# The first stage's steps put in other places within the engines' orders, its filler matmuls dropped, and the last 256 tokens stored in four pieces

## The chip, the cores and the metric

One core of a Trainium2 chip runs the kernel. The metric is device time in microseconds (us), the median of the timed runs. Engines: TensorE (PE, with its weight loads PEld), VectorE (DVE), ScalarE (ACT), GpSimd (POOL) and SyncE (SP), which issues most DMAs.

## The reference, cut to what matters

```python
# q, k, v: (4, 8, 576, 64); all float32
q_d, k_d, v_d = (t.reshape(B, H, 144, 4, D).mean(axis=3) for t in (q, k, v))
out_up = np.repeat(softmax_attention(q_d, k_d, v_d), 4, axis=2)
out_local = softmax_attention(q, k, v, mask=abs(i - j) < 4)
x = (out_up + out_local).transpose(0, 2, 1, 3).reshape(2304, 512)
h = np.maximum(np.maximum(x @ w1, x @ w2), x @ w3)      # 512 -> 768
x = h @ w_out                                           # 768 -> 512
h = x @ w_in; g = np.maximum(0.01 * h, h)               # 512 -> 2048
return g @ moe2_w_out                                   # 2048 -> 512
```

## The kernel before

Every product that needs full precision is done in parts: a value is split into a rounded high part and the rest (names ending in h and l), and three of the four partial products are summed.

The first stage makes the attention and the first mixture. It goes through eight units u of 288 tokens. For each unit TensorE runs 18 steps `L{u}.0` to `L{u}.17` (line 921, 12 matmuls of 288 columns each, into one PSUM bank out of a ring of four) and then eight steps `Y{u}.o.p` (line 953: four column blocks o; p = 0 has 15 matmuls and p = 1 the last three, which need `hl{u}.5`). Each L has an eviction `X` (ACT or DVE); after every third come `hh` and `hl`, the high and low part of the maximum (`hl` on POOL, in the last two units on DVE). A bank is free for the fourth allocation after it when its X is done.

Between these steps stand those of the attention. Units 0 to 3 use TensorE for the local part, per head pair h: `C{u}.h` scores (PE), `D` maximum (DVE), `E` exponentials (ACT), `H` reciprocal (DVE), `I` normalising (POOL), `O` transposes (PE), `o` copy (DVE), `P` product (PE), `Q` sum with the pooled part (DVE), `R` high part, `S` low part (POOL). `L{u}.0` needs `S{u}.3`. Units 4 to 7 do it without TensorE: products `mu` (POOL, 3.06 us each), sums `r` and `a` (DVE, ACT), softmax `s1`, `e`, `s2`, then `pm` and `ps` (DVE), and transposes `tp` with `ta`, `th`, `tx` behind them; `L{u}.0` needs `tx{u}.2`. The pooled attention of batch b has steps `A` (pooling), `B` scores, `F`, `G`, `J`, `K`, `PV`, `M` transposes, `m`, `N`, `v`. Until about 83 us DVE also joins the weights of the first mixture (`cy8` to `cy23`, two instructions each, with `cx`, `cz` on ACT or DVE and `cu` on POOL); a `cx` takes a bank of the ring of four too, which its `cy` gives back.

The second stage (lines 1148 and 1189, steps with @) is the second mixture: `@w..` split its weights, `@xl`, `@xs`, `@xh`, `@xo` load and split x, `@G` and `@H` are TensorE's steps, `@f..` add up the results, and `@fj`, `@fk` store them.

The order of all steps of one engine is fixed when the program is built: `Plan.order` (line 125) goes through the steps with planned durations and due times and returns one list; each engine works through its steps in the order of that list, whatever is ready. Two rules tie it to time. Where DVE works in a mode that shares its port with POOL (`Plan.alone`, line 121), the first such step waits for the last POOL step ahead of it in the list, and the other way round. And where the plan saw a gap of over 0.9 us on TensorE in its first 150 us (`KEEP_TO`), line 1682 put filler matmuls (`keep`, line 905) ahead of the step behind the gap. They write the unused columns of the bank of the newest L or Y step, with weights that compute nothing. Another 12 stand within `L0.0` (`FIRST`).

Of the kernel before, what the change touches and what calls it, by code (L numbers as in the profile page):

```python
# [19 lines left out]
DM = H * D  # L20
# [3 lines left out]
G = 32  # L24
# [9 lines left out]
M1 = FF1 // 128  # L34
M2 = FF2 // 128
# [9 lines left out]
N2 = 384  # L45
# [19 lines left out]
)  # L65
FILL0 = 7
FIRST = 12
KEEP_TO = 150.0
ON_A = (0, 21, 14)
NS = 3 * M1  # L70
CONV = 8
# [4 lines left out]
SHIFT = {"@": 8.7, "pv": 21, "ra": 7.2, "t": -44.8, "mu": 41.9, "c": 21.4, "ds3": -78.6, "ds2": -60.8, "pl3": -14.9, "pl1": 29.8, "co": 28.7, "pl2": 1.2, "ds1": -5.6}  # L76
SLACK = {"c": 20, "mu": 155.4, "ds3": 65.3, "co": -32.2, "t": 17, "pv": 57.9}
LEN = (56.8, 80.6, 38.5, 57.8, 38.8, 56.8, 30, 55)
GAP = 1.04
# [2 lines left out]
BANKS = {"B": "early", "M": "at", "N": "mm", "O": "at", "C": "early"}  # L82
BOOST = {"at": 36.8, "early": 10.6}


def kind(n):
    if n[0] == "@":
# [14 lines left out]
class Plan:  # L102
# [7 lines left out]
    def step(self, name, engine, time, fn, deps=(), after=0.2, alone=False, begin=-1e9, other=None):  # L110
        assert name not in self.steps
        self.steps[name] = dict(
            engine=engine, time=time, first=time, fn=fn, deps=list(deps), after=after, alone=alone, begin=begin, other=other, tags=[]
        )

    def holds(self, tag, bufs, first, last):
# [8 lines left out]
    def order(self, due, shift, slack, gap):  # L125
# [20 lines left out]
        for n in reversed(topo):  # L146
            due.setdefault(n, 1e9)
            for d in st[n]["deps"]:
                if n[0] == "@" != d[0]:
                    continue  # L150
                own = n[0] == "@" and st[d]["engine"] == st[n]["engine"]
# [3 lines left out]
        begin = {n: max(due[n] - slack.get(kind(n), 1e9), st[n]["begin"], FLOOR.get(kind(n), -1e9)) for n in due}  # L155
# [6 lines left out]
        out, now = [], 0.0  # L162
# [25 lines left out]
        while len(out) < len(st):  # L188
            began = False
            for e in self.ENGINES:  # L190
# [3 lines left out]
                for n, t in ready[e].items():  # L194
                    x = st[n]
# [9 lines left out]
                x = st[best]  # L205
# [21 lines left out]
            if not began:  # L227
# [28 lines left out]
def local_global_attention_moe_kernel(  # L256
# [14 lines left out]
    nc = tc.nc  # L271
    A, T = nc.scalar, nc.tensor
# [629 lines left out]
    def keep(n):  # L902
        w = ident.bitcast(BF16)
        for _ in range(n if "mm" in live and banks_taken[0] - live["at"] < 3 else 0):
            T.matmul(
                out=live["mm"][:, NCOL:], lhsT=w[:, :128], rhs=w[:, : 512 - NCOL],
                start=False, stop=False, skip_group_check=True,
            )
# [297 lines left out]
            fin[c, half] = p2["f"].tile([128, 2, 512], F32, tag="ob", bufs=3, name="ob")[:, : sups[c][1] // 256]  # L1206
        return fin[c, half][:, :, 256 * n : 256 * n + 256]

    def fin_store(c, half):
        n0, n = sups[c]  # L1210
        nt = n // 256
        for t in range(nt):
            store_rows(n0 + (half * nt + t) * 128, fin[c, half][:, t], A if half and c == len(sups) - 1 else nc.sync)

    def store_rows(first, ob, queue):
        a = 0
        while a < 4:
            u, r = divmod(first // G + a, RU)
            bb, half = divmod(u, 2)
            e = min(4, a + RU - r)  # L1220
            if u < PEU:
                row, step = first + a * G, DM
                runs = [(row, a, e)]
            else:
                row = u * NCOL + r if u == PEU and half else bb * S + half * RU + r
                step = (RU if u == PEU and half else R) * DM
                runs = [(row + x - a, x, x + 1) for x in range(a, e)]
            for row, x, y in runs:
                queue.dma_start(
                    out=bass.AP(tensor=out.tensor, offset=out.offset + row * DM, ap=[[step, (y - x) * G], [1, DM]]),  # L1230
                    in_=ob[x * G : y * G],
                )
            a = e
# [3 lines left out]
    with tc.manual_schedule(engines={ET.SP, ET.PE, ET.DVE, ET.Activation, ET.Pool}):  # L1237
# [408 lines left out]
        for c in range(len(sups)):  # L1646
            t = 0.16 + 0.54 * sups[c][1] / SB
            k = f"{c}"
            done = [f"@H{c}.{NP - 1}.{j}" for j in range(7)]

            def add(x, j, deps, f):
                go(f"@f{x}{k}", "DVE", t, f, deps)
                due[f"@f{x}{k}"] = due[done[j]] + 1.5

            go(f"@fa{k}", "ACT", t, lambda c=c: fin_copy(c, 0, "s1"), [done[0], "open6"])
            go(f"@fd{k}", "ACT", t, lambda c=c: fin_copy(c, 3, "s5"), [done[3]])
            due[f"@fa{k}"], due[f"@fd{k}"] = due[done[0]] + 1, due[done[3]] + 1
            add("b", 1, [f"@fa{k}", done[1]], lambda c=c: added(fin_ob(c, 0, 0), fin[c, "s1"], in_bank(c, 1)))
            add("c", 2, [f"@fb{k}", done[2]], lambda c=c: added(fin_ob(c, 0, 1), fin[c, "s1"], in_bank(c, 2)))
            add("e", 4, [f"@fc{k}", done[4]], lambda c=c: added(fin[c, "s1"], fin_ob(c, 0, 1), in_bank(c, 4)))  # L1660
            add("f", 5, [f"@fe{k}", done[5]], lambda c=c: added(fin_ob(c, 1, 0), fin[c, "s1"], in_bank(c, 5)))
            add("g", 6, [f"@fd{k}", f"@fe{k}"], lambda c=c: added(fin_ob(c, 0, 1), fin_ob(c, 0, 1), fin[c, "s5"]))
            add("h", 6, [f"@fg{k}", done[6]], lambda c=c: added(fin_ob(c, 0, 1), fin_ob(c, 0, 1), in_bank(c, 6)))
            add("i", 6, [f"@ff{k}"], lambda c=c: added(fin_ob(c, 1, 1), fin[c, "s1"], fin[c, "s5"]))
            go(f"@fj{k}", "SP", 1.45, lambda c=c: fin_store(c, 0), [f"@fb{k}", f"@fh{k}"], after=2.0)
            go(f"@fk{k}", "SP", 1.45, lambda c=c: fin_store(c, 1), [f"@ff{k}", f"@fi{k}"], after=2.0)
            due[f"@fj{k}"] = due[f"@fk{k}"] = due[done[6]] + 5
            for j, x in enumerate("abcdefh"):
                holds("yyyyxxz"[j], 4 if j < 4 else 2, f"@H{c}.0.{j}", [f"@f{x}{k}"])
            holds("s1", 1, f"@fa{k}", [f"@ff{k}", f"@fi{k}"])  # L1670
            holds("s5", 1, f"@fd{k}", [f"@fg{k}", f"@fi{k}"])
            holds("ob", 3, f"@fb{k}", [f"@fj{k}"])
            holds("ob", 3, f"@ff{k}", [f"@fk{k}"])
        ordered = mybir.DependencyInfo(mybir.DependencyClass.Sync, mybir.DependencyReason.DATA)
        apart = {"DVE": None, "POOL": None}
        done = 0.0
        for n in pn.order(due, SHIFT, SLACK, GAP):
            x = pn.steps[n]
            if x["engine"] == "PE" and n[0] != "@":
                gap = pn.end[n] - x["time"] - done  # L1680
                done = pn.end[n]
                if 0 < done < KEEP_TO and gap > 0.9:
                    keep(int((gap - 0.5) / 0.1))
            if x["engine"] not in ("DVE", "POOL") or n[0] == "@":
                x["fn"]()
                continue
            eng = V if x["engine"] == "DVE" else P
            eng.first, before = None, apart[x["engine"]]
            x["fn"]()
            if before is not None and (x["engine"] == "POOL" or pn.alone(n, "DVE")):  # L1690
                tc.add_manual_dep(eng.first.ins, before.ins.name, ordered, reason="one port")
                apart[x["engine"]] = None
            if x["engine"] == "POOL":
                apart["DVE"] = eng.last
            elif pn.alone(n, "DVE"):
                apart["POOL"] = eng.last
# [69 lines left out]
```

## Time and profile before

| what | value |
|---|---|
| median of 3 runs | 766.83 us (766.65 to 771.97) |
| the profiled execution, its time | 768.03 us |
| its span, first to last instruction | 766.2 us |
| PE busy | 753.7 us (98%) |
| DVE, ACT, POOL busy | 586.9, 442.2, 234.6 us |
| filler matmuls in all | 30 |

A row of the timeline gives start, duration, engine, line, operation, what is written and read, its size and count; in brackets stands the idle time of the engine before it and what ended it. Neighbours of one kind are merged. Line 248 is a helper through which all DVE and POOL operations go, so they are told apart by their tiles: `hm` is written by X, `wl` and `wy` by the joins cy, `ps_ls` and `plsm` by D and H, `dsqk` by A, `plt` by o, `hl` and `xl` by hl and S, `qkprod` by mu.

### The profile page before, as it was taken

How to read it: one execution, taken by the hardware profiler on the slowest of the kernel's cores; microseconds unless marked ns; L12 is line 12 of the kernel's file. 1: busy time of each engine (PE TensorE's matmuls, PEld its weight loads, DVE VectorE, ACT ScalarE, POOL GpSimd, SP SyncE). 2: the span in 40 equal slices, each digit the busy share in tenths (PEclk: the TensorE clock that was granted, in tenths of full speed). 3: DMA queues.
4: the chain of work that ended last, by engine and by line, in shares of the span. 5: the costliest groups of instructions: out<-in, count | busy, mean ns of one | idle time of the engine just before them, and what ended most of it. 6: DMA issues, size and time to landing. Idle time of an engine off the chain costs nothing.

```text
span 766.2 us, 16061 instructions
## 1 busy us (share of the span) xinstructions
PE 753.7 (98%) x5929; PEld 724.1 (95%) x5929; DVE 586.9 (77%) x1045; ACT 442.2 (58%) x1464; POOL 234.6 (31%) x221
## 2 busy tenths in 40 slices
PE   9999999999999999999999999999999999999997
PEld 5788899889899999999999999999999999999997
DVE  6998675577996893876788888668666987879882
ACT  6988549685246854223456798668678443433440
POOL 5988769787768855100000000000000000000000
PEclk9999999999999999999999999999999999999999
DMA  9972073645424203041324777987987545454522
GB/s 361 407 309 71 17 262 113 197 131 154 147 95 142 73 31 108 1 131 40 114 85 149 247 269 248 369 312 252 317 256 269 145 116 164 125 148 138 152 73 80
DMA packets 58510, 130.60 MB, mean 170 GB/s; under 512 B 5952, under 2 KB 30528, under 8 KB 58432
## 3 DMA queue, kind: packets, MB, share of 16 engines
q1 hardware_dynamic: 53680, 124.60, 48.6%
q10 hardware_dynamic: 4752, 4.98, 1.9%
q8 instruction: 46, 0.75, 0.4%
q14 instruction: 32, 0.26, 0.1%
HBM read 93.91 MB, written 35.65 MB: 169 GB/s over the span
## 4 chain that ended last, share of the span: by engine, by line
PE 79%; POOL 8%; DVE 6%; DMA 3%; issue 2%; ACT 2%; DVEq 0%; ACTq 0%; SPq 0%; POOLq 0%
PE acc L1189 22%; PE ps_h L921 19%; PE ps_y L1148 13%; PE ps_o L953 9%; PE ps_z L1148 7%; POOL qkprod L248 4%; PE ps_x L1148 3%; PE ps_sc L743 2%; DMA sqk<-in_qk_dram 1%; ACT qkprod L484 1%; POOL hl L248 1%; DMA lk<-in_kL_dram 1%; DVE wl L248 1%; POOL ple L248 1%; PE ps_ls L593 1%
## 5 line engine op out<-in xcount | busy, mean ns | idle before, releaser
L921 PE MATMUL ps_h<-xh,wA 128*128 128x288 f32 x1152 | 198.3, 299 | 0.2 <-ACT xh L391 0.2
L921 PEld LDWEIGHTS ps_h<-xh,wA 128*128 128x128 f32 x1152 | 166.4, 190 | 5.6 <-issue 3.7
L1189 PE MATMUL acc<-w,gs 128*128 128x256 f32 x1512 | 171.6, 276 | 0.0
L1189 PEld LDWEIGHTS acc<-w,gs 128*128 128x128 f32 x1512 | 171.5, 188 | 0.0
L921 PE MATMUL ps_h<-xl,wA 128*128 128x288 f32 x576 | 108.8, 295 | 1.1 <-POOL xl L248 1.0
L1148 PE MATMUL ps_y<-xop,w 128*128 128x384 f32 x576 | 105.7, 335 | 0.0
L1172 ACT ACTIVATE gs<-gr 128x1792 fp32r<-128x1792 f32 x36 | 60.8, 1703 | 76.0 <-DVE gr L248 61.8
L1148 PEld LDWEIGHTS ps_y<-xop,w 128*128 128x128 f32 x576 | 100.3, 188 | 0.1
L921 PEld LDWEIGHTS ps_h<-xl,wA 128*128 128x128 f32 x576 | 87.6, 190 | 1.8 <-POOL xl L248 1.8
L248 DVE TENSOR_TENSOR gs<-gr,gs 128x1792 fp32r<-128x1792 f32 x36 | 72.6, 2021 | 13.3 <-ACT gs L1172 13.2
L953 PE MATMUL ps_o<-hh,wO 128*128 128x288 f32 x384 | 79.0, 300 | 0.0
L248 POOL TENSOR_TENSOR qkprod<-lq,lk 128x1344 f32<-128x1344 f32 x24 | 73.7, 3081 | 4.9 <-issue 2.1
L484 ACT ACTIVATE qkprod<-qkprod 128x64 f32<-128x64 f32 x280 | 67.4, 255 | 6.5 <-POOL qkprod L248 4.9
L953 PEld LDWEIGHTS ps_o<-hh,wO 128*128 128x128 f32 x384 | 60.8, 188 | 2.1 <-issue 1.4
L248 DVE TENSOR_TENSOR gr<-gr 128x256 f32<-128x256 f32 (+1 forms) x108 | 53.3, 509 | 9.4 <-DMA gr<-gd 7.9
L248 DVE TENSOR_TENSOR hm<-hm,ps_h 128x288 f32<-128x288 f32 x96 | 42.9, 447 | 21.8 <-PE ps_h L921 20.2
L953 PE MATMUL ps_o<-hl,wO 128*128 128x288 f32 x192 | 56.4, 294 | 1.2 <-POOL hl L248 1.2
L484 ACT ACTIVATION_READ_ACCUMULATOR qkprod<-qkprod 128x1 f32 x280 | 56.2, 201 | 0.1
L1148 PE MATMUL ps_z<-xop,w 128*128 128x384 f32 x288 | 53.8, 335 | 0.0
L1148 PEld LDWEIGHTS ps_z<-xop,w 128*128 128x128 f32 x288 | 50.3, 188 | 0.0
L1131 ACT ACTIVATE g<-g 128x384 f32<-128x384 f32 x72 | 37.3, 521 | 20.9 <-DVE g L248 16.8
L248 DVE TENSOR_TENSOR w<-w2y,w 128x512 fp32r<-128x512 f32 (+1 forms) x64 | 38.5, 618 | 6.1 <-ACT w L1060 6.1
(143 smaller groups left out, 1194.6 us busy)
## 6 DMA issues: line engine op xcount, KB each, us to landing
gd<-g SPq DMA_DIRECT2D x96, 192.0 KB, 4.1
gr<-gd SPq DMA_DIRECT2D x32, 512.0 KB, 4.1
sqk<-in_qk_dram SPq DMA_DIRECT2D x20, 579.0 KB, 4.5
wA<-in_wa_dram SPq DMA_DIRECT2D x18, 512.0 KB, 9.8
dsrawv<-in_vP_dram SPq DMA_DIRECT2D x16, 512.0 KB, 3.9
wl<-in_w_in_dram SPq DMA_DIRECT2D x16, 512.0 KB, 3.3
wl<-in_w_out_dram SPq DMA_DIRECT2D x16, 512.0 KB, 4.7
wd<-w2y SPq DMA_DIRECT2D x8, 896.0 KB, 5.8
```

Source lines behind the costliest of these rows:

```text
L248: self.last = f(*args, **kwargs)
L484: A.activation(out=pr[:, r, j], in_=pr[:, r, j], func=AF.Copy, accum_out=sc[:, r, j : j + 1])
L593: T.matmul(out=pst[hh][:QB, j * KB : j * KB + KB], lhsT=qr[rows, qs], rhs=kr[rows, ks], start=False, stop=j == NBLK - 1,)
L743: T.matmul(out=pst[hh][:QC, c * SD : c * SD + SD], lhsT=t[rows, 0, qs] if b else raw[rows, qs, f], rhs=t[rows, 1, :], start=f == 0, stop=f ...
L921: T.matmul(out=ps, lhsT=wA[m, e][wi][:, kk * 128 : kk * 128 + 128], rhs=xx[:, kk], start=n == 0, stop=n == 3 * KC - 1)
L953: T.matmul(out=ps, lhsT=wO[m][wi][:, os_], rhs=xx[:, m], start=m0 == n == 0, stop=m1 == M1 and n == len(terms) - 1)
L1131: A.activation(out=g, in_=g if src is None else blk.pop((q, src)), func=AF.Prelu, alpha=0.01)
L1148: T.matmul(out=ps, lhsT=w[:, kk * 128 : kk * 128 + 128], rhs=xx, start=j in (0, 1, 3) and n == 0, stop=n == 5, skip_group_check=True,)
L1172: A.activation(out=ga[i][:, 0], in_=gr[i], func=AF.Copy)
L1189: T.matmul(out=acc[c, j][:, k * 256 : k * 256 + 256], lhsT=a[:, m : m + 128], rhs=w, start=p == 0 and k == 0 and n == 0, stop=p == NP - 1 ...
```

## The change

Steps stay what they are. After `Plan.order` a new method takes 838 steps out of the list and puts each run of them behind a named step (table `MOVED`, 251 runs), and gives 51 steps of copying or pooling to the other of their two engines (`SWAPPED`). The filler matmuls of `KEEP_TO` are gone (`KEPT` is empty); the 12 of `FIRST` stay. For the last 256 tokens each of the two stores is cut into two column halves: the first half is issued when its columns are done.

```diff
-KEEP_TO = 150.0
+MOVED = (
...
+    "H1.1>o1.0>hh0.3 C1.2>P1.0 cz16>cz15 cy17>X0.12 cu16>I1.1 L0.13>O1.1>D1.2>cy18>Q1.0>L0.14>cu15 "
...
+    "@w3i4.1>@xo0.1>@w0i5.0 @wqi5.0>Y7.0.0>Y7.1.0>Y7.0.1>st7.0>@w1i5.0 @w3i4>@wri5.0>Y7.2.0>Y7.1.1>Y7.3.0 "
...
+KEPT = {}
...
+    def rearrange(self, out):
+        runs = [r.split(">") for r in MOVED.split()]
+        moved = {n for r in runs for n in r[1:]}
+        out = [n for n in out if n not in moved]
+        for first, *rest in runs:
+            i = out.index(first) + 1
+            out[i:i] = rest
+        for n in SWAPPED.split():
+            x = self.steps[n]
+            x["engine"], x["time"] = x["other"] if x["engine"] == x["own"] else (x["own"], x["first"])
+        return out
...
-    def fin_store(c, half):
+    def fin_store(c, half, part=None):
...
+        c0, c1 = (0, DM) if part is None else (256 * part, 256 * part + 256)
...
+            store_rows(n0 + (half * nt + t) * 128, fin[c, half][:, t, c0:c1], A if half and part else nc.sync, c0, c1)
...
-        for n in pn.order(due, SHIFT, SLACK, GAP):
+        for n in pn.rearrange(pn.order(due, SHIFT, SLACK, GAP)):
             x = pn.steps[n]
-            if x["engine"] == "PE" and n[0] != "@":
-                gap = pn.end[n] - x["time"] - done
-                done = pn.end[n]
-                if 0 < done < KEEP_TO and gap > 0.9:
-                    keep(int((gap - 0.5) / 0.1))
+            if n in KEPT:
+                keep(KEPT[n])
```

Read out of the list before and the table, the orders of the places that the text below comes to:

```
PE, first unit    before: L0.0 C1.0 L0.1 .. L0.5 C1.1 L0.6 O1.0 L0.7 L0.8 L0.9 P1.0 L0.10 C1.2 L0.11 O1.1 ..
                  after:  L0.0 L0.1 C1.0 L0.2 .. L0.8 O1.0 C1.1 L0.9 L0.10 L0.11 L0.12 C1.2 P1.0 L0.13 O1.1 ..
                  before: .. L0.17 O1.2 B1.0 Y0.0.0 P1.2 ..    after: .. L0.17 P1.2 B1.0 Y0.0.0 ..
DVE, from L0.10   after:  X0.10 cy16 X0.11 cy15 H1.1 o1.0 hh0.3 cy17 D1.2 cy18 Q1.0 X0.13 cy19 H1.2 X0.14 o1.1
                          cy20 cy22 hh0.4 D1.3 cy21 Q1.1 o1.2 A1.0 H1.3 X0.16 X0.17
PE, around Y2     before: Y2.1.1 Y2.3.0 P3.3 N2.0 Y2.2.1 Y2.3.1 M2.1 B2.3 L3.0 ..
                  after:  Y2.1.1 N2.0 P3.3 Y2.3.0 Y2.2.1 Y2.3.1 M2.1 L3.0 L3.1 L3.2 L3.3 N2.1 L3.4 B2.3 ..
POOL, unit 1      before: I2.3 mu10.0 hl1.5           after: I2.3 S2.1 hl1.5 A2.0 .. S2.3 mu10.0
POOL, unit 2      before: mu11.0 S2.3                 after: S2.3 mu10.0 .. mu11.0
POOL, unit 3      before: K2.2 mu12.0 PV2.2 S3.3      after: mk11 S3.3 PV2.2 A2.3 hl3.0 K2.2 .. mu12.0
                  before: mu12.2 mu13.2 hl3.5         after: hl3.4 hl3.5 mu12.2 .. mu13.2
DVE, unit 7       before: X7.17 hh7.5 hl7.5
                  after:  X7.17 @wri4.1 @w2i4.0 @w2i4.1 @w5i26 @xo0.4 @w5i21 hl7.5   (hh7.5 on ACT)
```

## Rows read from the trace of the kernel before

**Rows 1.** Windows: stretch, its length, busy us (instructions) by engine, clock, DMA share, GB/s
```profile
42.40:80.40 38.00, 36.31 (x312) 33.97 (x313) 34.42 (x75) 33.23 (x97) 32.51 (x37) 1.00 0.38 148
203.80:207.50 3.70, 2.16 (x18) 1.35 (x16) 3.60 (x7) 1.82 (x6) 2.47 (x4) 0.89 0.51 151
207.50:210.10 2.60, 2.60 (x12) 2.60 (x12) 2.49 (x4) 0.00 (x0) 2.30 (x4) 0.51 0.27 101
415.70:595.00 179.30, 179.30 (x1049) 179.17 (x1049) 134.34 (x229) 136.58 (x274) 0.00 (x0) 1.00 0.81 278
```

**Rows 2.** Timeline of PE in unit 0: filler matmuls and the step behind them
```profile
59.21 0.54 PE L905 MATMUL ps_h<-ident 128*128 128x224 bf16 x4 [0.82 <-DVE hm L248]
...
80.41 1.12 PE L905 MATMUL ps_h<-ident 128*128 128x224 bf16 x10
...
82.10 0.40 PE L953 MATMUL ps_o<-hh,wO 128*128 128x288 f32 x1
```

**Rows 3.** Timeline of DVE in unit 0
```profile
58.71 0.45 DVE L248 TENSOR_TENSOR hm<-hm,ps_h 128x288 f32<-128x288 f32 x1
59.08 0.69 DVE L248 SCALAR_TENSOR_TENSOR wl<-wA,wl 128x512 int32<-128x512 int32 x1
...
60.78 1.37 DVE L248 TENSOR_REDUCE dsqk<-sqk 128x144 f32<-128x576 f32 x2
...
76.62 1.06 DVE L248 TENSOR_REDUCE ps_ls<-ps_ls 96x3 f32<-96x306 f32 x2
...
79.91 0.44 DVE L248 TENSOR_TENSOR hm<-hm,ps_h 128x288 f32<-128x288 f32 x1
...
81.01 0.78 DVE L248 COPY plt<-ps_lt 102x384 f32<-102x384 f32 x2
```

**Rows 4.** Timeline of PE from 144 to 247 us: the steps that waited
```profile
144.90 0.52 PE L953 MATMUL ps_o<-hh,wO 128*128 128x288 f32 x2
146.29 0.40 PE L953 MATMUL ps_o<-hl,wO 128*128 128x288 f32 x1 [0.88 <-POOL hl L248]
...
157.37 0.40 PE L921 MATMUL ps_h<-xl,wA 128*128 128x288 f32 x1 [0.15 <-POOL xl L248]
...
196.44 0.38 PE L645 MATMUL ps_lt<-ident,ple 96*102 96x96 f32 x2 [0.22 <-DVE dssum L248]
...
204.75 0.44 PE L791 MATMUL ps_aT<-ident,dse 72*72 72x72 f32 x4 [0.55 <-ACT up L391]
206.18 1.39 PE L743 MATMUL ps_sc<-dsqk 64*72 64x144 f32 x8 [0.99 <-ACT aT L391]
...
246.85 0.40 PE L953 MATMUL ps_o<-hl,wO 128*128 128x288 f32 x1 [0.32 <-POOL hl L248]
```

**Rows 5.** Timeline of POOL: what stood ahead of hl1.5, S3.3 and hl3.5
```profile
141.34 3.06 POOL L248 TENSOR_TENSOR qkprod<-lq,lk 128x1344 f32<-128x1344 f32 x1 [0.42 <-DVE hh L248]
...
205.10 0.80 POOL L248 TENSOR_TENSOR xl<-x,xh 128x288 fp32r<-128x288 f32 x1 [0.18 <-ACT xh L391]
...
239.90 6.14 POOL L248 TENSOR_TENSOR qkprod<-lq,lk 128x1344 f32<-128x1344 f32 x2
```

**Rows 6.** Timeline of PE in units 5 and 6: a whole L step, and the first L of unit 6
```profile
320.17 1.22 PE L921 MATMUL ps_h<-xh,wA 128*128 128x288 f32 x8
...
321.75 1.21 PE L921 MATMUL ps_h<-xh,wA 128*128 128x288 f32 x8
...
338.88 0.65 PE L921 MATMUL ps_h<-xh,wA 128*128 128x288 f32 x3
```

**Rows 7.** Timeline of DVE: the last low part for unit 6, and hl7.5
```profile
337.19 0.29 DVE L248 TENSOR_TENSOR xl<-ps_x,xh 128x128 fp32r<-128x128 f32 x1 [0.44 <-ACT xh L882]
...
407.05 0.46 DVE L248 TENSOR_TENSOR hl<-hm,hh 128x288 fp32r<-128x288 f32 x1
```

**Rows 8.** Timeline of PE in Y7.0.1: its first matmul with hl7.5
```profile
410.23 0.29 PE L953 MATMUL ps_o<-hl,wO 128*128 128x288 f32 x1
```

**Rows 9.** DMA issues of the last 12 us: tiles, queue, count, size, us to landing
```profile
out_dram<-ob SPq DMA_DIRECT2D x1, 256.0 KB, 2.4
```

More of the change, by code (lines that the diff above doesn't have):

```diff
@@ L86, in kind @@
+SWAPPED = (
[3 rows of a table added]
+)
+KEPT = {}
 def kind(n):
@@ L112, in step @@
         self.steps[name] = dict(
-            engine=engine, time=time, first=time, fn=fn, deps=list(deps), after=after, alone=alone, begin=begin, other=other, tags=[]
+            engine=engine, own=engine, time=time, first=time, fn=fn, deps=list(deps), after=after, alone=alone, begin=begin, other=other, tags=[]
         )
@@ L1207, in fin_ob, with store_rows @@
         return fin[c, half][:, :, 256 * n : 256 * n + 256]
-    def fin_store(c, half):
+    def fin_store(c, half, part=None):
         n0, n = sups[c]
         nt = n // 256
+        c0, c1 = (0, DM) if part is None else (256 * part, 256 * part + 256)
         for t in range(nt):
-            store_rows(n0 + (half * nt + t) * 128, fin[c, half][:, t], A if half and c == len(sups) - 1 else nc.sync)
-    def store_rows(first, ob, queue):
+            store_rows(n0 + (half * nt + t) * 128, fin[c, half][:, t, c0:c1], A if half and part else nc.sync, c0, c1)
+    def store_rows(first, ob, queue, c0, c1):
         a = 0
@@ L1229, in store_rows @@
                 queue.dma_start(
-                    out=bass.AP(tensor=out.tensor, offset=out.offset + row * DM, ap=[[step, (y - x) * G], [1, DM]]),
+                    out=bass.AP(tensor=out.tensor, offset=out.offset + row * DM + c0, ap=[[step, (y - x) * G], [1, c1 - c0]]),
                     in_=ob[x * G : y * G],
@@ L1664, in local_global_attention_moe_kernel @@
             add("i", 6, [f"@ff{k}"], lambda c=c: added(fin_ob(c, 1, 1), fin[c, "s1"], fin[c, "s5"]))
-            go(f"@fj{k}", "SP", 1.45, lambda c=c: fin_store(c, 0), [f"@fb{k}", f"@fh{k}"], after=2.0)
-            go(f"@fk{k}", "SP", 1.45, lambda c=c: fin_store(c, 1), [f"@ff{k}", f"@fi{k}"], after=2.0)
-            due[f"@fj{k}"] = due[f"@fk{k}"] = due[done[6]] + 5
+            for x, half, deps in (("j", 0, "bh"), ("k", 1, "fi")):
+                deps = [f"@f{y}{k}" for y in deps]
+                if c == len(sups) - 1:
+                    for part in range(2):
+                        go(f"@f{x}{k}" if part else f"@f{x}{k}.0", "SP", 0.75, lambda c=c, h=half, p=part: fin_store(c, h, p), [deps[part]], after=2.0)
+                        due[f"@f{x}{k}" if part else f"@f{x}{k}.0"] = due[done[6]] + 5 if part else due[deps[0]] + 1
+                else:
+                    go(f"@f{x}{k}", "SP", 1.45, lambda c=c, h=half: fin_store(c, h), deps, after=2.0)
+                    due[f"@f{x}{k}"] = due[done[6]] + 5
             for j, x in enumerate("abcdefh"):
@@ L1675, in local_global_attention_moe_kernel @@
         apart = {"DVE": None, "POOL": None}
-        done = 0.0
-        for n in pn.order(due, SHIFT, SLACK, GAP):
+        for n in pn.rearrange(pn.order(due, SHIFT, SLACK, GAP)):
             x = pn.steps[n]
-            if x["engine"] == "PE" and n[0] != "@":
-                gap = pn.end[n] - x["time"] - done
-                done = pn.end[n]
-                if 0 < done < KEEP_TO and gap > 0.9:
-                    keep(int((gap - 0.5) / 0.1))
+            if n in KEPT:
+                keep(KEPT[n])
             if x["engine"] not in ("DVE", "POOL") or n[0] == "@":
```

69 lines of the change are left out of this document (added), and 3 rows, old and new, of the table SWAPPED.

## The prediction

> **What bounds the kernel now.** I read the page first (TensorE is busy for 98% of the span), then the windows by stretch, then TensorE's timeline wherever a window shows less than its full length, and last the timelines of the engines that ended its waits. From 415.70 to 595.00 TensorE is busy for 179.30 of 179.30 us at full clock [rows 1]: the second stage has nothing that an order could win. What can be won lies in the first stage, in two kinds of places.
>
> The first is unit 0. From 42.40 to 80.40 VectorE is busy for 34.42 of 38.00 us [rows 1], with the joins of the weights between TensorE's evictions. In this stretch the fillers cost time. They write the bank that the last L has just filled, so they cannot start until its eviction has read it: the eviction that starts at 58.71 ends at 59.16, and the fillers start at 59.21; the one at 79.91 ends at 80.35, and the ten fillers start at 80.41 [rows 2, 3]. The reader is to see that a filler meant for an idle gap here makes the gap.
>
> The second are single waits between 144 and 247 us [rows 4]. `hl1.5` came late for Y1.0.1: two matmuls from 144.90, the third at 146.29. At 0.132 us a matmul (12 from 320.17 to 321.75 [rows 6]) the two need 0.26, so 1.13 us are lost where the row says 0.88 idle; a wait costs some 0.25 more than its idle time, since a matmul's drain counts as busy. In the same way `S2.3` cost 0.15 + 0.25 = 0.40, a bank for `O3.3` 0.22 + 0.25 = 0.47, and `hl3.5` 0.32 + 0.25 = 0.57. The largest place is M2.1 and B2.3: idle for 0.55 and 0.99, with the same addition 2.04. Behind it the granted clock was 0.51 for the 2.60 us from 207.50 [rows 1], that is 1.2 of 2.4 GHz, which cost about 1.3.
>
> **The change, part by part.** *The waits from 144 to 247 us.* Ahead of `hl1.5` on GpSimd stood a product of 3.06 us, ahead of `hl3.5` two of together 6.14 [rows 5]; both now stand behind it, and the same is done for `S2.3`. Ahead of `S3.3`, which ran at 205.10, one product and two shorter steps go. Each of these moves more than the wait it answers. B2.3 reads banks that M2.1's copies must first give back, and stood directly behind it; now five L and a small step lie between, 5 x 1.58 = 7.9 us against a wait of 0.99. N2.0, whose copy (the ACT `up` of the 0.55) M2.1 waited for, goes ahead of P3.3 and Y2.3.0; that step's 15 matmuls (15 x 0.132 = 2.0) cover 0.55. With the waits the fall of the clock goes, as TensorE was idle just before it. I take all of it: 1.13 + 0.40 + 0.47 + 2.04 + 1.3 + 0.57 = 5.9 us gained; the bounds are 0 and 5.9.
>
> *Unit 0.* Without the fillers' wait L0.9 can start 0.82 + 0.25 before 59.21, at 58.15, and with P1.0 moved behind it L0.10 ends 2 x 1.58 later, at 61.3. From there VectorE sets the pace, since the banks for the next L come from its joins. Ahead of B1.0 it has, in the new order: 8 joins at 1.39 (from 59.08 to 60.47 as the sum of two of 0.69), 11.1; 11 small steps (evictions, Q, H, two hh) at 0.37 (58.71 to 59.08), 4.1; two D at 1.06, 2.1; three o at 0.78, 2.3; A1.0, 1.37 [rows 3]. Together 21.0, so to 82.3. B1.0 itself takes what is left between 80.41 and 82.10 when ten fillers of about 0.1 are taken off (1.12 for all, most of it overlapped), some 0.65; so Y0.0.0 starts at about 83.0 instead of 82.10 [rows 2]. But P1.2 then lies behind TensorE and M1.1 stands later: two steps like B1.0, some 0.5 each, estimated from it. So unit 0 gains nothing: -0.9 + 1.0, which I take as 0. The bounds: VectorE waits as long again as it was idle before (38.00 - 34.42 = 3.6), of which some 1.5 fall on TensorE's path: -1.5; or TensorE sets the pace and the three filler groups' 2 x (1.07 + 0.3) + 1.0 come back: +3.7.
>
> *Unit 7.* `hl7.5` now has six weight steps ahead of it. It ran at 407.05 [rows 7], and its first reader at 410.23 [rows 8], a cover of 410.23 - 407.51 = 2.7. Six steps of about 0.6 (a 0.69 instruction starts every 0.6 to 0.7, as joins do [rows 3]) are 3.6, and hh7.5's 0.3 leaves VectorE: hl7.5 is ready at 410.8, so Y7.0.1 waits 0.6. Loss 0.6, bounds 0 and 1.5. What queues behind hl7.5 on VectorE are steps for `@G`, all wanted after 415.70.
>
> *The swaps* move steps of 0.3 to 0.45 between VectorE and ScalarE and are in the counts above where they lie in unit 0. *The table's DMAs* (73 of the moved steps are SP's) issue loads behind others that wait for their buffer; I take 0.3 lost in all for products that start later on GpSimd, which had the room.
>
> *The last stores.* A store of 256 KB took 2.4 us to land [rows 9]; the last pieces are now 128 KB. If half of it went with the bytes, 1.2 would go; if nothing did, 0. I take 0.3, near the lower end, because the piece still has to be issued and confirmed. [...]
>
> The sum: 5.9 + 0 - 0.6 - 0.3 + 0.3 = 5.3 us. The profiled execution took 768.03, so its like would take 762.7; the median of the runs is 766.83, 1.2 lower, and by it 761.5.
>
> **The rivals.** *Everything goes, unit 0 too.* TensorE then gains up to 3.7 more there; with 3 of it the time is 758.5. For it speaks that the fillers' wait is real [rows 2, 3]; against it that VectorE has 21 us of work where TensorE has less.
>
> *The gain is given back at L6.0.* GpSimd's products are put off, not saved, and units 4 to 7 hang on them and on VectorE. `L6.0` started at 338.88, the last low part that it needs ended at 337.48 [rows 6, 7]: only 1.4 us of cover. If VectorE does not get to that part earlier, all gain beyond 1.4 ends there: 1.4 - 0.6 + 0.3 = 1.1, so 765.7. Against it speaks that the transposes for it stand between TensorE's own steps and move with them.
>
> *Slower: the clock falls in unit 0.* With no fillers TensorE stands still in some six places between 61 and 83 us, as it did for 0.55 and 0.99 before the clock fell at 207 [rows 1, 4]. TensorE has about 16 us of work there (7 x 1.58 and some 5 of small steps) in 21.7; at half clock that is 32, or 10 late: 761.5 + 10 = 771.5, slower than before. A fall as long as the one in the trace, 2.60 us in that window, hides in the 5.7 us that VectorE leaves; it decides against the change from 5.7 + 5.3 = 11 us of work at half clock on. The Trainium skill (TensorE: Matmul & The Clock Gate, "Part 1: The HAM clock gate") says that half clock is the resting state and that the engine's own activity releases it; by that page fillers are what keeps it, and the one fall in the trace, behind the idle 0.55 and 0.99, agrees. Against it speaks that TensorE was busy for 36.31 of 38.00 in this stretch at clock 1.00, three waits included [rows 1].
>
> **How the numbers follow.** The forecast (759.2 to 764) 0.46; all of it gained (757 to 759.2) 0.29; given back at L6.0 or at another wait of that kind (764 to 767) 0.17; the clock or another new wait in unit 0 (767 to 776) 0.08. The range leaves out the last case and the outer part of the second: 757.5 to 766.5. About 1% is what a measurement of this kernel can tell from no change, so faster begins at 759.2 and slower at 774.5: faster 0.29, within 0.67, slower 0.04 (half of the last case).
>
> **What would show it.** Right: no L905 rows behind 45 us; no idle of TensorE put down to a POOL `hl` or `xl` between 140 and 250; B2.3 without a wait and the clock at 1.00 around L3.0; Y0.0.0 at 82 to 83.5 with waits for VectorE of 0.3 to 1.5 ahead of it; Y7.0.1 waiting for a VectorE `hl`; the second stage starting 5 to 6 us before 415.70 with no idle in it. Wrong: Y0.0.0 well before 82 (unit 0 pays), L6.0 waiting for `xl` (given back), a clock of 0.5 between 61 and 83, or waits of the second stage's first steps for weights that the table puts later.

## The result, and the profile after

The kernel after takes 777.93 us (median of four, 776.93 to 780.33) against 768.08 for the kernel before: a ratio of 1.0125, 95% interval 1.0078 to 1.0171. It is slower by about 10 us where a gain of 5.3 was forecast. Its profiled execution took 776.93 us with a span of 775.1; before it was 768.03 with 766.2. Code behind the table stands 90 lines lower in after (L921 is L1011, L1189 is L1279). Below, the steps `@G` are called the second stage and the steps `@H` the third; the text so far counts both to the second.

The two traces are best compared by the starts of TensorE's steps, in us:

| step | before | after | after minus before |
|---|---|---|---|
| Y0.0.0, first product of unit 0 | 82.10 | 83.21 | +1.1 |
| L1.0 | 97.74 | 97.14 | -0.6 |
| L4.0 | 253.07 | 243.65 | -9.4 |
| L5.0 | 295.26 | 288.84 | -6.4 |
| L7.0 | 377.58 | 372.78 | -4.8 |
| G0.0.0, start of the second stage | 415.52 | 411.29 | -4.2 |
| G0.1.3, its eighth step | 422.80 | 425.04 | +2.2 |
| H0.0.0, start of the third stage | 590.36 | 593.05 | +2.7 |
| last matmul | 761.63 | 771.01 | +9.4 |
| end of the span | 766.16 | 775.14 | +9.0 |

So the first stage did gain, more than forecast up to L4.0. Then 3.0 us go in unit 4, 6.5 in the first seven steps of the second stage, and 6.7 in the third stage, whose matmuls the change does not touch.

The windows of after (stretch, length, busy us and instructions of PE, PEld, DVE, ACT, POOL, clock, DMA share, GB/s). The first answers the first of [rows 1]. The second is the stretch from L1.0 to L4.0: no idle time, and the clock, which in before fell around L3.0, stays at 1.00:

```profile
42.40:80.40 38.00, 34.56 (x296) 31.80 (x295) 32.71 (x71) 32.05 (x94) 26.87 (x24) 1.00 0.33 127
97.14:243.65 146.51, 146.51 (x1277) 138.90 (x1276) 109.22 (x221) 87.68 (x544) 110.86 (x100) 1.00 0.42 141
244.00:256.00 12.00, 9.50 (x71) 8.69 (x70) 4.24 (x10) 6.10 (x43) 7.89 (x6) 1.00 0.91 335
411.30:416.00 4.70, 3.29 (x20) 2.96 (x18) 2.35 (x4) 0.61 (x2) 0.00 (x0) 1.00 0.85 262
418.00:424.00 6.00, 4.88 (x15) 4.57 (x15) 6.00 (x11) 4.59 (x10) 0.00 (x0) 0.50 0.12 41
600.00:750.00 150.00, 150.00 (x1276) 150.00 (x1275) 121.86 (x154) 57.49 (x41) 0.00 (x0) 1.00 0.46 132
```

The same stretch of the third stage in before:

```profile
600.00:750.00 150.00, 150.00 (x1326) 150.00 (x1325) 125.63 (x157) 58.41 (x40) 0.00 (x0) 1.00 0.45 130
```

In both TensorE is busy for 150.00 of 150.00 us at clock 1.00 and waits for nothing, yet it ran 1326 matmuls in before and 1276 in after. From the first start to the last of the 1512 matmuls it is 171.28 us in before, 0.1133 us each, and 177.96 in after, 0.1178 each: 6.7 us. A share of busy time can't show this; the count can.

TensorE's timeline in after at the places of [rows 2] and [rows 8], and where it newly waited:

```profile
83.21 0.53 PE L1043 MATMUL ps_o<-hh,wO 128*128 128x288 f32 x2
...
250.37 0.79 PE L1011 MATMUL ps_h<-xh,wA 128*128 128x288 f32 x4 [1.48 <-ACT ev L1050]
...
253.62 0.68 PE L833 MATMUL ps_sc<-dsqk 64*72 64x144 f32 x6 [1.01 <-DVE xl L338]
...
405.91 0.40 PE L1043 MATMUL ps_o<-hl,wO 128*128 128x288 f32 x1 [0.32 <-DVE hl L338]
...
416.82 1.50 PE L1238 MATMUL ps_x<-xop,w 128*128 128x384 f32 x6 [2.23 <-ACT ev L1050]
419.43 4.21 PE L1238 MATMUL ps_y<-xop,w 128*128 128x384 f32 x12 [1.12 <-ACT p L1209]
```

Two of the new waits end at ScalarE's `ev`, the eviction of a finished first-stage product (`st`). ScalarE's own timeline says why it was late (ACTq is its queue issuing the store):

```profile
243.46 0.41 ACT L1050 ACTIVATE ev<-ps_o 128x288 f32<-128x288 f32 x1 [1.50 <-PE ps_o L1043]
243.90 0.35 ACTq L1051 DMA_DIRECT2D x2d<-ev  x1
244.35 0.41 ACT L1050 ACTIVATE ev<-ps_o 128x288 f32<-128x288 f32 x1 [0.48 <-ACT ev L1050]
244.80 0.33 ACTq L1051 DMA_DIRECT2D x2d<-ev  x1
249.91 0.41 ACT L1050 ACTIVATE ev<-ps_o 128x288 f32<-128x288 f32 x1 [5.14 <-DMA x2d<-ev]
...
411.09 0.41 ACT L1050 ACTIVATE ev<-ps_o 128x288 f32<-128x288 f32 x1 [0.24 <-PE ps_o L1043]
411.53 0.35 ACTq L1051 DMA_DIRECT2D x2d<-ev  x1
411.93 0.41 ACT L1050 ACTIVATE ev<-ps_o 128x288 f32<-128x288 f32 x1 [0.43 <-ACT ev L1050]
412.37 0.33 ACTq L1051 DMA_DIRECT2D x2d<-ev  x1
416.35 0.41 ACT L1050 ACTIVATE ev<-ps_o 128x288 f32<-128x288 f32 x1 [4.01 <-DMA x2d<-ev]
```

The tile `ev` has two buffers (`bufs=2`). The table puts st3.2, st3.3 and st3.1 in a row, and st7.2, st7.1 and st7.3. The third of each must wait until the first one's store has landed: from the issue at 243.90 to 249.91, and from 411.53 to 416.35. ScalarE stands still meanwhile (5.14 and 4.01 us), and as it works in the order of its list, everything behind it is late: at 250 us the banks for L4.3 and the `xh` that `xl` is made from, at 416 us the bank for G0.1.1 and the copies `p` for G0.0.2. Behind the wait of 2.23 us the granted clock fell as well: 0.50 from 418.00 to 424.00, that is 1.2 of 2.4 GHz. The 12 matmuls from 419.43 took 4.01 us to the next step, at 423.44, where 12 such take 2.08 in before; in all the half clock makes some 2.4 of the 6.5 us, and the two waits the rest.

The price in unit 4 is not a fixed one. In the five profiled kernels that keep the table's evictions (after, e3_fill, e4_whole, e5_base, e9_gap) it is 45.2 to 48.0 us from L4.0 to L5.0, in the five with the table that do not keep them 41.99 each time.

The last stores, answering [rows 9]:

```profile
out_dram<-ob SPq DMA_DIRECT2D x3, 128.0 KB, 1.8
out_dram<-ob ACTq DMA_DIRECT2D x1, 128.0 KB, 1.8
```

### The profile page after: what moved, and what is told of

Its sections match the earlier page's. It is cut to its first block, busy times and chain, and to the rows that moved or that the text cites. A ratio compares the mean times of both kernels' runs of the same rounds, so it can differ in the third digit from the quotient of the medians.

```text
span 775.1 us, 15992 instructions
## 1 busy us (share of the span) xinstructions
PE 758.2 (98%) x5907; PEld 730.0 (94%) x5911; DVE 584.1 (75%) x1032; ACT 446.3 (58%) x1477; POOL 234.4 (30%) x221
## 4 chain that ended last, share of the span: by engine, by line
PE 89%; DVE 4%; ACT 3%; DMA 2%; issue 1%; POOL 1%; ACTq 0%; DVEq 0%; POOLq 0%
PE ps_h L1011 27%; PE acc L1279 23%; PE ps_y L1238 13%; PE ps_o L1043 9%; PE ps_z L1238 7%; PE ps_x L1238 3%; PE ps_sc L833 2%; DMA x2d<-ev 1%; PE ps_ls L683 1%; PE ps_up L902 1%; PE ps_aT L881 1%; ACT qkprod L574 1%; PE ps_lo L756 1%; DVE wl L338 1%; PE ps_lt L735 1%
## 5 line engine op out<-in xcount | busy, mean ns | idle before, releaser
L1011 PE MATMUL ps_h<-xh,wA 128*128 128x288 f32 x1152 | 195.5, 298 | 2.7 <-ACT ev L1050 1.5
L1279 PE MATMUL acc<-w,gs 128*128 128x256 f32 x1512 | 178.2, 281 | 0.0
L1279 PEld LDWEIGHTS acc<-w,gs 128*128 128x128 f32 x1512 | 178.2, 189 | 0.0
L1011 PEld LDWEIGHTS ps_h<-xh,wA 128*128 128x128 f32 x1152 | 165.4, 189 | 7.4 <-issue 2.1
L1238 PE MATMUL ps_y<-xop,w 128*128 128x384 f32 x576 | 107.9, 340 | 1.1 <-ACT p L1209 1.1
L1011 PE MATMUL ps_h<-xl,wA 128*128 128x288 f32 x576 | 108.1, 293 | 1.0 <-POOL xl L338 0.9
L1238 PEld LDWEIGHTS ps_y<-xop,w 128*128 128x128 f32 x576 | 102.2, 191 | 1.6 <-ACT p L1209 1.6
L1011 PEld LDWEIGHTS ps_h<-xl,wA 128*128 128x128 f32 x576 | 87.1, 189 | 1.4 <-POOL xl L338 1.4
L574 ACT ACTIVATION_READ_ACCUMULATOR qkprod<-qkprod 128x1 f32 x280 | 54.0, 193 | 0.0
```

The lines of the kernel that those rows point to most:

```text
L574: A.activation(out=pr[:, r, j], in_=pr[:, r, j], func=AF.Copy, accum_out=sc[:, r, j : j + 1])
L1011: T.matmul(out=ps, lhsT=wA[m, e][wi][:, kk * 128 : kk * 128 + 128], rhs=xx[:, kk], start=n == 0, stop=n == 3 * KC - 1)
L1238: T.matmul(out=ps, lhsT=w[:, kk * 128 : kk * 128 + 128], rhs=xx, start=j in (0, 1, 3) and n == 0, stop=n == 5, skip_group_check=True,)
L1279: T.matmul(out=acc[c, j][:, k * 256 : k * 256 + 256], lhsT=a[:, m : m + 128], rhs=w, start=p == 0 and k == 0 and n == 0, stop=p == NP - 1 ...
```

## The experiments

**Which part costs what: stores alone, fillers back, whole stores.** The first takes only the four-piece stores into the kernel before:

> The kernel before with the four-piece stores alone; no step of the first stage is moved. Theory of the result (ev): the stores end the span about 0.5 us sooner behind the last matmul (4.57 us in the trace of before, 4.09 in that of after), so 766 to 768 us and nothing else changes. On the pace of the third stage, where before had 0.1133 us from matmul to matmul and after 0.1178: if the pace belongs to the order of the program (theory P-program), it is 0.1133 here; if it falls by chance in each execution (theory P-chance), it can be either, and 0.1178 throughout would make the time 773 us.

Measured: 767.77 us, ratio 0.9994 (0.9974 to 1.0014). The third stage kept its 0.1133 us. From the last matmul's start to the end of the span it is 3.84 us, where before has 4.52.

```diff
-KEPT = {}
+KEPT = {"L0.9": 4, "L0.14": 4, "B1.0": 10}
```

> The kernel after with the 18 filler matmuls of before put back: 4 ahead of L0.9, 4 ahead of L0.14, 10 ahead of B1.0. Theory: VectorE sets the pace of the first unit and the fillers stand in time that TensorE has to spare, so Y0.0.0 starts at 83.2 us as in after (82.1 in before) or up to 1 us later, and the time is 777 to 779 us. If the count of TensorE's instructions ahead of the third stage decided its pace (5561 matmuls in before, 5543 in after), it is 0.1133 us here and the time 771 us; by chance per execution it can be either.

Measured: 779.55 us, half a microsecond over the expectation. Y0.0.0 started at 86.06, where the nine kernels with the table and without fillers have 83.1 to 83.9. The fillers cost over 2 us in the new order, more than expected. The third stage stayed at 0.1178, so the count of instructions ahead of it isn't what sets its pace.

> The kernel after with the last 256 tokens stored in two whole pieces, as before; all steps of the table stay. Theory: the span ends 0.5 us later behind the last matmul than in after, so 778 to 779 us if the pace of the third stage belongs to the program (0.1178, as in after: the code up to there is the same). If the pace falls by chance in each execution, 0.1133 is to be seen in this or another run of the batch, and the time can be 772 us.

Measured: 778.01 us, third stage 0.1178, and 4.83 us from the last matmul's start to the end of the span (4.12 in after). The stores are worth 0.7 us in both pairs of traces, too little for these times to resolve. The slow pace comes with the table: the four kernels seen with it so far (after, e2_st, e3_fill, e4_whole) had 0.1178, the two without it 0.1133.

**The evictions.**

```diff
+BACK = (("st3.0", "Y3.2.0"), ("st3.1", "Y3.3.0"), ("st7.0", "Y7.2.0"), ("st7.1", "Y7.3.0"), ("st7.2", "Y7.3.1"), ("st7.3", "st7.2"))
...
+        for n, x in BACK:
+            out.remove(n)
+            out.insert(out.index(x) + 1, n)
```

> The kernel after, with only six evictions of the last first-stage product moved back to the places they have in before: st3.0, st3.1 and st7.0 to st7.3. Theory ev (three evictions in a row share two buffers, so the third waits on ScalarE for the first one's store to land, 5.1 and 4.0 us): no wait of ScalarE for a store of x2d is left, the waits of TensorE at 247 to 254 us (3.1 us) and at 413 to 425 us (about 6 us) go, the second stage starts near 408 us instead of 411.3 and the third near 584 instead of 593. At the pace 0.1178 the time is then 768 to 770 us, at 0.1133 it is 761 to 763. Rival (ScalarE's load: the weight steps that the table puts among the evictions make it late): the waits stay, at 775 to 778 us.

Measured: 772.53 us, 5.4 below after, ratio to before 1.0059 (1.0037 to 1.0081). ScalarE's timeline in unit 3 shows no wait for a store:

```profile
239.25 0.41 ACT L1054 ACTIVATE ev<-ps_o 128x288 f32<-128x288 f32 x1 [1.69 <-PE ps_o L1047]
...
241.72 0.41 ACT L1054 ACTIVATE ev<-ps_o 128x288 f32<-128x288 f32 x1 [2.06 <-PE ps_o L1047]
...
244.38 0.40 ACT L1054 ACTIVATE ev<-ps_o 128x288 f32<-128x288 f32 x1
...
245.23 0.41 ACT L1054 ACTIVATE ev<-ps_o 128x288 f32<-128x288 f32 x1 [0.46 <-ACT ev L1054]
```

From L4.0 to L5.0 it is 41.99 us (45.19 in after, 42.19 in before), so theory ev holds in unit 4. At the second stage it held by half. These are the waits there, in us in total, times, longest:

```profile
ACT ev L1054 <- DMA x2d<-ev: 2.9, 1, 2.9
...
PE ps_y L1242 <- ACT p L1213: 2.4, 1, 2.4
```

The evictions still came in a burst, because a weight step ahead of st7.0 holds ScalarE for 3.02 us, and `p` stands behind six more weight steps. So there the rival, ScalarE's load, had its part. The time is 2.5 us over the top of what was expected at this pace.

The profile names no releaser for the 3.02 us, and the expectations of e8_late and e12_start below put them down to the step's load. The traces speak against that: the load landed at 403.14 at the latest, and the step starts at 404.57, 0.09 us after VectorE has ended the `w` steps that read the older `w2y` (at 404.48; the gap is 0.09 in after too). The program makes it wait for that VectorE step. `w2y` has two buffers, like `ev`, and here a third fill waits for the last reader again:

```profile
403.20 1.28 DVE L342 TENSOR_TENSOR w<-w2y,w 128x512 fp32r<-128x512 f32 x2
...
404.57 0.67 ACT L1105 ACTIVATE w2y<-wl 128x512 f32<-128x512 f32 x1 [3.02 <-issue]
```

**The pace of the third stage.** In both kernels the third stage has the same instructions on operands at the same addresses. What differs lies before it. Each tile xop is 6336 bytes, 24 x 256 + 192, so five of them set aside in the order 0, 1, 2, 3, 4 start at 192, 128, 64, 0, 192 modulo 256, and line 53 counts on this when it places the operands: `X2_BASE = (192, 128, 64, 0, 192, 64, 0)`. A tile gets its place at its first use. The table moves the preparations `@xh0.j` to the order 0, 3, 4, 2, 1, so tiles 1 to 4 trade places. Undone in after:

```diff
+        for j in (0, 1, 2, 3, 4):
+            xop0[j] = p2["x"].tile([128, 4 * N2 + 48], F32R, tag=f"xop{j}", bufs=1, name="xop")
```

> The kernel after with one thing undone: the five operand tiles xop0 to xop4 of the second stage are set aside in the order 0, 1, 2, 3, 4 when their pool opens, as before used them first, so that they lie where they lay in before. In after the table moves their preparations to the order 0, 3, 4, 2, 1, which swaps the places of four of them: they start 64 or 128 bytes off (modulo 256) from where X2_AT wants them. No step moves. Theory address (the places of the second stage's operands set its pace and leave TensorE in the slower pace of the third): the second stage runs at 0.1734 us from matmul to matmul instead of 0.1741 to 0.1747, the third at 0.1133 instead of 0.1178 throughout, 6.8 us less, and the time is 769 to 771 us. Rival (something else of the table's order sets the pace): 0.1178 stays and the time is 777 to 778 us.

And done to before, with the order (0, 3, 4, 2, 1):

> The kernel before with one thing done: the tiles xop0 to xop4 are set aside in the order 0, 3, 4, 2, 1, so that the second stage's operands lie exactly where they lie in after. No step moves and no wait is added. Theory address: the second stage's pace goes to 0.1741 to 0.1747 us for its first two thirds (about 0.5 us more), the third stage's to 0.1178 us (6.8 us more), and the time is 774 to 776 us. Rival (the table's order): the paces stay 0.1734 and 0.1133 and the time is 767 to 769 us.

Measured: e5_base 770.48 us, ratio to before 1.0020 (1.0005 to 1.0035), 7.5 below after; e6_shift 775.45 us, 1.0086 (1.0062 to 1.0111). The chain of work that ended last (start, us, line, count) has one row for nearly the whole third stage. In e5_base, at after's order with before's places:

```profile
594.62 170.05 PE acc L1283 x1500
```

In e6_shift, at before's order with after's places:

```profile
591.29 176.68 PE acc L1193 x1500
```

That is 0.1133 and 0.1178 us a matmul. The theory of the places holds both ways: they alone make 7 to 7.5 us of the loss, without a step moved or a wait added. It is not chance from execution to execution either: the ten of e5_base all lie at 771.71 or below, the four of e6_shift all at 774.77 or above. Most of the second stage, which reads these tiles, lost little: 168.01 us from G0.1.3 to H0.0.0 in after, 167.56 in before.

**Is the pace carried over?** One added VectorE instruction makes TensorE wait at the start of the third stage. (The VectorE step `@c42.7` goes ahead of it, by which 336 of the 1512 matmuls, from the 349th on, write another PSUM bank.)

```diff
+            if n == "@H0.0.0":
+                g = ga[0][:, 1, 0, 0:64]
+                V.tensor_tensor(out=g, in0=g.bitcast(F32), in1=g.bitcast(F32), op=ALU.max)
```

> The kernel after with one VectorE instruction added that makes the third stage's first matmul wait: a maximum of 64 columns of the first operand with themselves, placed behind the VectorE step that takes the last result of the second stage. The operand tiles stay where the table puts them (the slow case). TensorE stands still for about 1 to 2 us between the stages. Theory carried-over (the pace of the third stage depends on how TensorE comes out of the second, without a break): after the break the pace is 0.1133 us and the time 771 to 773 us. Rival (it is set by something that a break does not change): 0.1178 us, 778 to 780 us.

Measured: 775.27 us (two executions), between the two expectations. TensorE waited 1.2 us for `gs`, behind its first two matmuls, and then ran at 0.1133 us, the tiles being where the table puts them, until it had to wait for VectorE once more:

```profile
598.00 2.21 PE L1281 MATMUL acc<-w,gs 128*128 128x256 f32 x17 [1.20 <-DVE gs L340]
...
752.07 5.16 PE L1281 MATMUL acc<-w,gs 128*128 128x256 f32 x41 [0.32 <-DVE ob L340]
```

Behind this second break it ran at 0.1178 to the end. So a break can settle the pace anew, in either direction. It need not: in e10_mix, below, a wait of 0.16 us for `ob` at the same matmul left the fast pace as it was. The same break in the kernel before:

> The kernel before with the break of e9_gap ahead of the third stage: the same added VectorE instruction, and TensorE waits for it about 1.5 us. The operand tiles stay in their good places. If a break always leads to the fast pace, or the good places keep it, the third stage runs at 0.1133 us and the time is 769 to 771 us. If a break draws the pace anew, it can be 0.1178 us and 776 to 777 us.

Measured: 769.45 us median of eight executions, of which two took 774.63 and 775.97 us and six 767.61 to 769.86. The profiled one is that of 774.63. TensorE waited 0.57 us, again behind its first two matmuls, and ran at 0.1178 from there (the wait in its timeline, then the row of the chain):

```profile
590.50 3.68 PE L1189 MATMUL acc<-w,gs 128*128 128x256 f32 x29 [0.57 <-DVE gs L248]
```

```profile
590.50 176.71 PE acc L1189 x1498
```

So after a break one program can run at either pace, if the six shorter executions, which were not profiled, had the fast one, as their times say. Without a break, all eight kernels up to e6_shift gave the pace that goes with their places, and so did e7_all, e8_late, e10_mix and e12_start below, with the places of before and 0.1133 us.

**A version with all three mends:** the evictions as in e2_st, the places as in e5_base, and ScalarE's `p` ahead of weight steps.

```diff
+    ("@w4i30", "st7.3"), ("@p10.0", "@G0.0.1"), ("@w4i32", "@p10.0"), ("@p10.1", "@G0.1.1"), ("@w4i34", "@p10.1"))
```

> The kernel after with three mends together: the operand tiles back in their places (as in e5_base), the six evictions back in theirs (as in e2_st), and at the start of the second stage ScalarE's steps in the order of before: w4i30, p10.0, w4i32, p10.1, w4i34. Theory: e2_st's span of 771.2 us, less the 2.4 to 4.2 us that the first four G steps wait there for p10, less 6.8 us of the third stage's pace and some 0.5 us of the second's: 759 to 762 us, about 1% faster than before. If the pace is not a matter of the places: 766 to 768 us. If p10 was not what held the second stage: 763 to 766 us.

Measured: 765.57 us, ratio 0.9964 (0.9949 to 0.9979): faster than both kernels, but 3.6 us over the top of the expectation and within that of its second rival (p10 was not what held the second stage). G0.0.0 started at 408.54 and G0.1.3 at 417.25, 8.71 us where before needed 7.28, and one more wait followed:

```profile
PE ps_y L1247 <- ACT u L1218: 2.2, 2, 1.9
PE ps_y L1247 <- ACT p L1218: 1.2, 1, 1.2
```

The second stage's start is held by ScalarE. Two attempts to clear its queue followed. One moved the weight steps behind `u20.1` as a block, the other spread them out:

> The kernel e7_all with ScalarE's and VectorE's preparation of the second stage's later weights (all steps @w... that the table puts between the last first-stage products and the fourth G step) moved as one block behind the step u20.1, and hl7.5 put right behind hh7.5. Theory (what still holds the second stage's start in e7_all is ScalarE's queue: a weight step that waits 3.0 us for its load ahead of st7.0, then four evictions in a burst, then p10 and u20 behind weight steps): st7.0 runs when Y7.0.1 ends, no eviction waits for a store, the waits at p10 and u20 (1.2 and 1.9 us in e7_all) go, and Y7.2.0 no longer waits 0.6 us for hl7.5: 3 to 4.5 us less than e7_all's 765.6, so 761 to 763 us, unless the weights moved come too late for the G steps of the next pairs (then waits of TensorE for VectorE's w at 430 to 480 us, and 763 to 767 us). Rival (VectorE or the loads of the weights hold the start, not ScalarE): 764.5 to 766 us.

> The kernel e8_late with the weight steps not moved as one block but one or two at a time between the other steps behind u20.1, over the next 34 of these; the two loads w0i5.0 and w0i5.1 stay where the table has them. In e8_late the first seven G steps ran without a wait (7.28 us from G0.0.0 to G0.1.3, as in before), and then ScalarE stood in the block, for 2.2 us at a load and 3.9 us at VectorE, with u20.2 behind it: TensorE lost 8.8 us at G0.0.5 to G0.0.6. Theory: with the block spread out that wait goes and the early start of the second stage (407.95 us; 415.52 in before) lasts to the end: e8_late's 769.9 us less 8 to 8.8 us, 761 to 762 us, about 0.8 to 0.9% faster than before. Rival (the weights of the next pairs then come too late in other places): 764 to 767 us.

Measured: 769.90 us (1.0029) and 771.52 us (1.0044), slower both than e7_all and before, and outside all that was expected. In e8_late the first seven G steps did run in 7.28 us from 407.95 on, and hl7.5 cost nothing. But then ScalarE stood at steps whose inputs came late, and TensorE behind it. ScalarE's timeline in e8_late:

```profile
417.12 0.66 ACT L1111 ACTIVATE w2y<-wl 128x512 f32<-128x512 f32 x1 [2.23 <-DMA wl<-in_w_in_dram]
...
425.33 0.66 ACT L1111 ACTIVATE w2y<-wl 128x512 f32<-128x512 f32 x1 [3.87 <-DVE w L346]
```

VectorE's timeline there:

```profile
424.83 0.42 DVE L346 TENSOR_TENSOR w<-w2y,w 128x256 fp32r<-128x256 f32 x1
```

The rivals had the mechanism, if not the time: a weight passes load, ScalarE, VectorE, ScalarE and VectorE in turn. The wait of 2.23 us is for the load, which was put off with the rest. The one of 3.87 is for a buffer again: the step fills a third `w2y`, of which there are two, and starts when VectorE has read the oldest, at 425.25. In e10_mix the longest wait for `u` was 7.1 us. The last version moves only what stood in the way:

```diff
+    ("hl7.5", "hh7.5"), ("@wqi5.0", "st7.1"), ("@w1i5.0", "@wqi5.0"), ("@wri5.0", "@w1i5.0"),
+    ("@w5i32", "@c10.1"), ("@w5i28", "@w5i32"), ("@w5i30", "@w5i28"), ("@w3i5.0", "@w5i30"), ("@w0i6.0", "@w3i5.0"), ("@w0i6.1", "@w0i6.0"))
```

> The kernel e7_all with the start of the second stage put in a better order, and no weight step moved by more than a few places: ScalarE's first weight step wqi5.0 (which waits 3.0 us for its load there) and w1i5.0 go behind st7.1, so that the first two evictions run when their products are done; VectorE's w5i32, w5i28, w5i30 and w3i5.0 go behind c10.1; hl7.5 goes right behind hh7.5. Theory (ScalarE's eviction burst and VectorE's three w5 steps ahead of c10.0 are what is left at the start): no eviction waits for a store (2.8 us in e7_all), the waits of TensorE for p10 (1.2 us), u20 (1.9 us) and hl7.5 (0.6 us) go, and the time is 2.5 to 4 us below e7_all's 765.57: 761.5 to 763 us, 0.6 to 0.8% faster than before. Rival (the weights' own chain of load, ScalarE and VectorE is the bound, as e8_late and e10_mix showed where it is put off further, and the wait goes to the next step that needs ScalarE): 764.5 to 768 us.

Measured: 763.82 us, ratio 0.9939 (0.9920 to 0.9958). The second stage starts at 407.63 and the third at 586.00, 4.4 us sooner than in before. Of the new waits of TensorE behind 395 us one kind is left, 2.4 us:

```profile
PE ps_y L1249 <- ACT u L1220: 2.4, 2, 1.2
```

This beats both kernels: with the table's order, its losses undone and some ten steps of the second stage's start put elsewhere, 0.6% can be had.

## Why the prediction was wrong, point by point

**The waits from 144 to 247 us: right.** All waits of [rows 4] are gone and so is the half clock around 207.50. From L1.0 to L4.0 it is 146.51 us against 155.33, a gain of 8.8 where the term said 5.9. The named places gave the 5.9, if each matmul's distance from the one before is taken over the usual distance: 1.15 (`hl1.5`) + 0.42 (`S2.3`) + 0.38 (`O3.3`) + 0.71 and 1.00 (M2.1, B2.3) + 1.62 (half clock) + 0.59 (`hl3.5`). Some 0.6 more is work that the table moves behind L4.0, and no gain. Most of the other 2.3 are pauses of 0.1 to 0.2 us, which the term left out: TensorE goes from one kind of step to another 86 times instead of 100.

**Unit 0: the time right, the reading half right.** Forecast was Y0.0.0 at 83.0, measured 83.21, and 0 net at its end; measured is 0.6 gained at L1.0, of which 0.2 lies ahead of L0.0. (In e1_stores, with the order of before, L0.0 to L1.0 took 1.4 us longer than in before, so single executions differ here by more than that.) TensorE does wait: it is busy for 34.56 us of the window of 38.00 (36.31 in [rows 1]). But VectorE sets the pace for only half of the way. The chain that ended last goes through VectorE from 61.40 to 69.93, then through ScalarE until 78.39, and then through two instructions of VectorE (start, us, engine, what):

```profile
69.23 0.70 DVE wy L338
69.95 0.64 ACT wl L495
...
77.82 0.53 ACT wO L481
78.39 0.71 DVE wl L338
```

And the window of both engines from there to Y0.0.0:

```profile
61.00:83.20 22.20, 18.76 (x171) 16.14 (x169) 20.21 (x46) 19.70 (x63) 17.49 (x17) 1.00 0.08 25
```

ScalarE had 19.70 us of work there, nearly as much as VectorE's 20.21. The sum of VectorE's steps alone came out at the right time partly by luck. The clock stayed at 1.00, so the rival that it falls in unit 0 didn't happen; it fell behind 417 us, behind other waits.

**Unit 7: right.** Forecast 0.6 lost for hl7.5, measured 0.58 (10.08 us from Y7.0.0 to G0.0.0, 9.50 in before).

**The last stores: sized low.** 0.3 forecast, 0.7 in both pairs of traces. Between before and after 0.4 of it is left; the table costs the rest (4.83 us behind the last matmul's start in e4_whole, 4.52 in before).

**The step that failed first: "moved" was costed by engine and time, not by buffer.** The prediction asked of each moved step what engine it waits for and what stands behind it. It didn't ask whose buffer the step needs and when the buffer's last reader, a DMA, is done. The evictions `st` have two buffers and a store behind each, and the table moves 18 of 32 of them. The weight steps that fill `w2y` are a second such pair of buffers. Cost: 3.0 us in unit 4 and, with ScalarE's order and the half clock, 6.5 at the start of the second stage. Here the sum had 0.3 for "the table's DMAs", as loads waiting for their buffer, and nothing for a ScalarE step that waits for its own store.

**The step that failed second: "the second stage has nothing that an order could win".** It had no idle time to win, but some to lose: the 105 steps `@` that the table moves belong to it. The prediction put a start 5 to 6 us earlier with no idle in it; the start came 4.2 us earlier, and 6.5 were lost in the first seven steps. A stage that starts earlier also needs its preparation earlier, and ScalarE, which does much of it, had no such lead; this reason is argued, not tested by itself. Of the wrong signs that the prediction listed, "waits of the second stage's first steps" came true, though for evictions and copies rather than for weights. The rival that the gain is given back at L6.0 named the wrong place: L6.0 started 5.0 us sooner than before.

**The step that wasn't there: the places of tiles.** Nothing in the prediction asked what else an order of steps decides. A tile's place was decided by it, and line 53 of the kernel counts on the places. This is 6.7 us in the third stage and 0.5 in the second, and the largest single part. It could have been read from the diff: `@xh0.0`, `@xh0.3`, `@xh0.4`, `@xh0.2`, `@xh0.1` stand in the table in this order.

In sum, from the table of steps: -0.6 - 8.8 + 3.0 + 1.6 (units 5 and 6) + 0.6 + 6.5 + 0.5 + 6.7 - 0.4 = +9.0 us (each term is rounded). The 1.6 us of units 5 and 6 are in every kernel with the table. Some 1.4 of it is work moved there from unit 4: eight more matmuls that write `ps_up` and eight more that write `ps_aT` lie between L5.0 and L7.0 than in before.

## What to carry to other kernels

When steps are moved, go through each moved step's buffers as well as its engine: how many buffers the tile has, who reads them last, and how long a store takes to land where the DMA engines are busy. (A third buffer for `ev`, the other remedy here, was not tried.) Look for what the order decides besides time, such as places that are given out at first use, and set these aside in a fixed order if anything depends on them. Compare counts of instructions per stretch and not only busy shares: a stage can be 100% busy in both traces and 4% slower.

## What the runs showed of the hardware

The same matmul (128 x 128 by 256 columns, fp32r), at the same clock and addresses and without a wait, ran at one of two steady paces for 150 us and more: 0.1133 or 0.1178 us from start to start. Without a break, which of the two was settled at the start of the stage: in before five starts 0.119 to 0.123 us apart and then 0.1133 to the end, in after 0.115 to 0.119 from the first on. It depended on where the operands of the stage before lay, and a break of 0.3 to 1.2 us could settle it either way. The Trainium skill (TensorE: Matmul & The Clock Gate, "Wait — 56ns, not 53.3ns?") gives the columns at 2.4 GHz and some 2.5 ns more; that makes an estimate of 0.109 us here. Both paces measured lie above it, so the measurement decides. What inside TensorE keeps the pace, and which of the four moved tiles it takes, is open.

A store of 144 KB took 1.9 us to land in the median of after's 32, but about 6 us at 243.90, where the DMA engines were 0.91 busy, and 4.7 at 411.53, where they were 0.85 busy. The Trainium skill (DMA: Bandwidth & Descriptors, "Anatomy of one DMA — SWDGE (gpsimd) path") gives about 2.0 us that are fixed and a rest that goes with the size, for DMAs that GpSimd issues. The last stores, which SyncE and ScalarE issue, took 1.7 us for 64 KB, 1.8 for 128, and 2.1 (ScalarE's) and 2.4 for 256: the smaller ones lie below the page's fixed part, so for these queues the measurement decides.
